# Transposes of four attention slots on 64x64 quarters of TensorE, in another written-out order, in a retention-and-FFN kernel

## The chip, the cores and the metric

The kernel runs on one core of one Trainium2 chip. The metric is the device time of one execution in microseconds; the median of several runs is compared. TensorE is called PE, the loading of its weights PEld, VectorE DVE, ScalarE ACT, GpSimd POOL and SyncE SP, as in the profile.

## What is computed

A causal retention layer is followed by a feed-forward layer. For each of 4 batches and 8 heads (sequence 768, head size 64), with gamma = 1 - 2^(-5-h) for head h:

```python
for t in range(S):
    state = gamma * state + outer(k[t], v[t])
    y[t] = scale * (q[t] @ state)          # scale = 1/8
```

The eight heads of a token side by side are a row x of 512. With 3072 such rows, h = x @ w_in (512 by 2048), g = h * cos(h), and the result is g @ w_out (2048 by 512), in float32.

## The kernel before

The recurrence is done in chunks of 128 tokens. A *slot* p is one chunk of two batches; there are 12 slots, in the order of `ORDER`, and two slots make a *group* of 512 token rows for the FFN (6 groups). A slot goes through these steps:

- *Loads*: q, k and v of the slot, by DMA; those of slots 0 to 7 and the FFN weights (w_in in parts w0a, w0b, w1, w2, w3a, w3b; w_out in o0 to o3) are issued on POOL in the order of the list `LOADS` (q2 is q of slot 2).
- *Conversions* to bf16, with the decay factors multiplied in: q on POOL or DVE (L324, names cq20, cq21 for the two batches of slot 2), k on ACT (L313, ck20), v on POOL or DVE (L336, cv20).
- *Transposes* of q and k, because the scores need the head size on the partitions. Slots 0 to 5 do them on PE (`t_mm`, L361, names t20, t21) and copy them from PSUM to SBUF (`t_copy`, names eq20, ek20); later slots by DMA on SP (`dma_t`, names dt60, dt61). A half u of a slot is four heads, and has one PSUM bank.
- *Scores* (`a_mm`, L389, names a20 and a21 for the two halves of heads in slots 2 and 3, a4; for later slots inside the Y block of the slot before) and their masks (L408).
- *Y block* (`y_block`, L494, L480, L508): scores by v, q by the state, and the update of the state. It is issued on 64x64 quarters of PE, four matmuls side by side. Half of it has to wait for the other half[...]; `told` lets an engine given by `hop_on(p)` wait for the first half and signal the second. That engine is SP for slots up to 4 and POOL after.
- *x copies* (names yc20, yc21) into the 512-row tile `xt`.

The FFN of a group has 16 units of four matmuls (L590, 512 columns; `f_mm`, named f0.3), each followed by a cosine on ACT (L598) and a product on DVE (L602). Where only one slot of a group is ready, half units of 256 columns work on two columns of w_in at once (L611, `h_mm`, named h2.4). `HALF0` is the number of w_in columns of group 0 that are done in half units. `o_mm` (L635) multiplies by w_out.

From slot 6 on the order is a fixed loop (`for g in range(2, NG + 1)`). Before it, in the first 70 us or so, the order of all engines is made at build time by the class `Plan`: each step is added with the engines it may use, its assumed cost, what it follows, a rank, and tokens for PSUM banks and buffers; the plan then steps through time and gives each free engine the ready step of lowest rank. `SHIFT` adds to the ranks of named steps, `ON` limits engines, and both are tables of numbers found by a search. `HOLD` names engines that rather wait than begin a step when one of much lower rank is about to be ready. Where PE would have nothing in the first 18 us, a filler matmul on zeros (L664) is put. The resulting order is emitted instruction by instruction; at run time each engine keeps its order and waits by semaphore.

Of the kernel before, what the change touches and what calls it, by code (L numbers as in the profile page):

```python
# [164 lines left out]
HOLD = ""  # L165
SHIFT = {"ml010": 25.5, "mulf0.2": -74.7, "f0.3": 0.3, "cosf0.2": -11.6, "cosf0.3": -2.2, "mulf0.3": -4.9, "f0.2": 2.8, "m011": -20.0, "mulh1.4": -20.5, "m000": 82.7, "cosf0.5": -41.6, "ck21": 45.1, "a31": -124.5, "m100": 2.2, "f0.5": 23.0, "a5": -2.5, "v0": -97.2, "ms110": 6.4, "ml110": -41.8, "cosf0.4": -0.9, "f0.4": -9.8, "mulf0.5": 16.9, "eq51": 13.1, "m110": 64.4, "t20": -21.1, "k5": -46.0, "mulf0.8": 31.6, "yc21": -50.4, "f0.6": 2.1, "f0.7": 55.3, "ek10": -92.1, "w0b": -22.2, "a21": -34.2, "h1.0": 81.4, "cosh2.2": 3.0, "m501": 38.5, "yc30": -23.3, "ml011": -27.8, "mulf0.15": 5.8, "sc5": 79.1, "m201": -81.3, "mulh2.2": -18.0, "oc1": -45.8, "mulf0.14": -66.8, "cq31": -32.2, "mulf0.9": -47.9, "mulf0.6": 5.7, "cosf0.7": -27.8, "a30": -8.1, "cosf0.6": -7.2, "h0.2": -12.1, "eq21": -4.6, "cq51": 3.2, "cq41": 38.6, "f0.14": 23.8, "ek20": -13.4, "yc50": 39.8, "cv51": 23.4, "ek51": 88.5, "mulh2.10": 23.3, "cq70": 8.6, "f0.10": -46.0, "mulf0.13": 1.5, "h1.6": 5.9, "ml100": 20.1, "f0.15": 60.8, "o2.1": -8.1, "h3.10": 31.9, "t51": 14.8, "h3.0": -7.1, "h3.14": 28.8, "cq00": -2.7, "m601": 4.7, "h1.4": 1.8, "eq11": 37.0, "cosf0.12": -60.7, "v6": -26.4, "m400": 17.7, "mulh3.12": 67.0, "w2": 49.4, "sw": -53.6, "cv10": -0.0, "rv00": 14.5, "mulh2.8": 4.5, "ek50": 72.2, "cosf0.11": 2.4, "m101": -34.4, "h2.2": 1.1, "q2": -22.9, "q5": -59.7, "cosh3.14": 19.9, "y3": 19.8, "t40": 30.7, "o2": -0.8, "mulh3.4": -0.3, "cq40": -13.2, "mulh0.2": -29.3, "y5": -35.7, "mulh3.14": -25.5, "h2.12": -50.9, "oc0": -94.2, "a10": 39.9, "ek11": -35.3, "h0.6": 6.9, "eq40": -6.2, "h2.6": 58.1, "rv10": -9.1, "dt71": -1.3, "cosh3.8": -31.0, "cosh0.2": 18.8, "cv70": -67.6, "o3.1": -13.8, "cq60": -11.1, "ck60": 71.1, "m511": 10.9, "sc4": -15.9, "o1.3": -16.8, "m510": 4.5, "k4": 12.5, "h0.4": -9.2, "cq71": 3.6, "mulh3.2": 58.9, "cosh1.2": -26.7, "mulh3.6": -1.4, "cv61": 13.7, "o2.2": -9.8, "q6": -7.4, "o0.2": -7.5, "mulh2.4": 44.5, "mulh2.6": 22.6, "mulh3.10": 16.6, "v5": -53.7, "cq61": 27.8, "o1.1": -27.2, "ck61": 0.2, "m200": -10.8, "cosf0.9": 6.3, "cosh0.4": 11.6, "q4": 78.9, "cosh3.6": -6.8, "h1.2": -87.9, "tq01": 1.8, "oc3": -74.8, "mulh0.0": -16.9, "eq01": 11.2, "t21": 6.2, "ck41": 29.7, "cosh3.4": 9.3, "oc2": 8.6, "m211": 23.9, "cq01": -56.9, "w0a": 17.8, "o1.0": -7.7, "yc01": 2.2, "k7": 54.8, "yc51": -0.7, "cosf0.13": -14.9, "cosh2.10": -36.4, "yc00": 7.1, "cosh1.4": -13.4, "ek00": -8.7, "m611": -13.9, "tk10": -101.4, "mulh0.4": -40.7, "mulf0.10": 15.2, "m600": -35.2, "a00": -17.4, "cosh2.0": -5.5, "m301": 18.6, "rv11": -50.0, "sc0": -52.0, "ek01": -31.6, "cv01": 13.3, "ek21": -3.2, "cosf0.10": 7.2, "v7": -2.1, "ek40": 18.1, "t31": 22.7, "mulh1.6": 0.2, "eq30": -9.4, "y4": 19.2, "tk11": 1.9, "ek31": -26.9, "w3b": 23.5, "cosh2.12": -0.2, "cosh0.6": 4.7, "cosh2.8": -4.4, "cosh3.2": 25.8, "cv60": 2.7, "cosh2.4": -14.4, "v4": -1.1, "mulh2.12": 36.6, "dt61": -8.8, "eq41": -12.5, "mulf0.11": 31.8, "ek41": -0.8, "eq50": 9.1, "a11": -23.9, "yc10": 9.3, "o0.3": 0.3, "dt60": -3.3, "o3.3": 50.5, "mulh2.14": -42.3, "m610": -12.1, "f0.11": -0.6, "s0": 3.1, "cv11": 38.9, "h3.8": -17.4, "yc40": 14.3, "m410": -8.4, "h2.8": -4.0, "m300": 15.8, "o0": -14.6, "cv31": -27.4, "rv01": 0.6, "cosf0.14": 2.4, "cosh2.6": 11.7, "cv50": -6.8, "m010": -1.2, "ms011": -12.0, "f0.13": -5.2, "l8": 5.1, "ck70": 3.2, "t41": 1.0, "o1.2": -2.3, "cv71": 0.5, "tq11": 31.2, "h2.4": -3.6, "mulh0.6": 8.8, "t50": 7.1, "ck31": 42.7, "yc20": -52.3, "m001": -4.7, "y01": 62.0, "y2": 15.3, "f0.12": 20.5, "ms111": 2.0, "mulh1.2": -13.9, "cosh3.10": -49.0, "ck51": -9.0, "h0.0": -0.1, "eq31": 1.4, "eq20": -5.1, "q7": 1.5, "cosh3.0": 6.2, "cosh3.12": 1.5, "cv40": 2.3, "y11": 3.6, "o1": -24.4, "cv00": -1.4, "sc2": -3.2, "m411": 18.0, "m210": -8.1, "v3": 0.0, "eq10": 1.1, "tk01": 22.8, "yc41": -25.6, "cq21": -1.8, "f0.9": -31.4}
ON = {"cv70": "P", "cv00": "D", "cv30": "D", "cv31": "D", "cv60": "D", "cv11": "D", "cv10": "P", "rv01": "D", "sc5": "D", "rv11": "A", "yc20": "D", "sc3": "D", "eq40": "DA", "eq50": "A", "rv00": "A", "yc00": "D", "yc31": "DA", "ek51": "D", "ek11": "DA", "sc4": "D", "ek20": "A", "cv61": "P", "eq01": "DA", "cv51": "D", "ek41": "D", "eq41": "A", "cv20": "P", "yc01": "DA", "eq20": "A", "eq30": "DA", "ek50": "D", "ek00": "D", "sc2": "DA", "yc50": "DA", "yc40": "A", "yc21": "A", "cq21": "D", "ek40": "DA", "cv01": "D", "cv71": "P", "cv21": "P", "ek21": "DA", "cv41": "P", "cq20": "D", "ek10": "DA", "yc30": "A", "ek01": "D"}
HALF0, SPARE, RF, RM, COLD = 8, 1, 50.0, 50.0, 5.2
# [3 lines left out]
def kernel(  # L172
# [9 lines left out]
    nc = tc.nc  # L182
# [15 lines left out]
    SWAP = 8  # L198
    LATE = NC
# [61 lines left out]
    def qb(p):  # L261
        return by_b(qs[p % NB], p)

    def kb(p):
        return by_b(kx if p == 1 else ks[p % NB], p)
# [89 lines left out]
    def t_mm(p, u, w):  # L355
        if w == 0:
            held["t", p, u] = banks.take()
        tr = held["t", p, u].bitcast(BF16).rearrange("p (w a t) -> p w a t", w=2, a=HP)
        for a in range(HP):
            x = (kb(p) if w else qb(p))  # L360
            nc.tensor.transpose(  # L361
                tr[:, w, a, :],
                x[:, u, 2 * a : 2 * a + 2, :] if p < 2 else x[:, :, 4 * u + a, :], ident)

    def t_copy(p, u, w, e):
        bank = held["t", p, u]
        tr = bank.bitcast(BF16).rearrange("p (w a t) -> p w a t", w=2, a=HP)
        copy(e, qkt[p % NB][:, w, ts(u, HP), :], tr[:, w])
        if w == 1:
            banks.give(bank)  # L370
# [96 lines left out]
    def hop_on(p):  # L467
        return nc.sync if p <= 4 else nc.gpsimd
# [238 lines left out]
    CQ, CD = "P", "DP"  # L707
    SPLIT = {(1, 1, 1), (0, 1, 1)}
    HM, HCQ, HCV = "q2", "", ""
# [9 lines left out]
    LOADS = ["Q1", "K1", "v0", "v1", "w0a", "w0b", "w1", "w2", "q2", "k2", "w3a", "v2", "w3b", "o0", "q3", "k3", "v3", "o1", "q4", "o2", "k4", "v4", "q5", "k5", "o3", "v5", "q6", "k6", "v6", "q7", "k7", "v7"]  # L719
# [28 lines left out]
    for p in range(PL + 2):  # L748
# [26 lines left out]
        if p < DMA_T:  # L775

            for u in range(2):
                cq, ck = ([T["c" + x, p, b] for b in ((u,) if p < 2 else (0, 1))] for x in "qk")
                ev = lambda w, x, need: add("DA", SB2, lambda e, p=p, u=u, w=w: t_copy(p, u, w, e),
                                            need + old, 10 * p + 0.5, (), [("bank", 1)] if w else [],  # L780
                                            name="e%s%d%d" % (x, p, u))
                if p < 2:
                    tq = add("E", 0.225, lambda e, p=p, u=u: t_mm(p, u, 0), cq, 10 * p + 1,
                             [("bank", 1)], (), "full", name="tq%d%d" % (p, u))
                    T["eq", p, u] = ev(0, "q", [tq])
                    tk = add("E", 0.225, lambda e, p=p, u=u: t_mm(p, u, 1), ck + [T["eq", p, u]],
                             10 * p + 1, (), (), "full", name="tk%d%d" % (p, u))
                    T["ek", p, u] = ev(1, "k", [tk])
                else:
                    tq = tk = add("E", 0.45, lambda e, p=p, u=u: (t_mm(p, u, 0), t_mm(p, u, 1)),  # L790
                                  cq + ck, 10 * p + 1, [("bank", 1)], (), "full",
                                  name="t%d%d" % (p, u))
                    T["eq", p, u] = ev(0, "q", [tq])
                    T["ek", p, u] = ev(1, "k", [tk, ("issued", T["eq", p, u])])
                T["tq", p, u], T["tk", p, u] = tq, tk
# [202 lines left out]
```

## Time and profile before

| what | value |
|---|---|
| median of 4 runs | 208.67 us (208.31 to 209.05) |
| profiled execution | 208.43 us, its span 206.6 us |
| PE busy | 201.9 us (98%), 2178 matmuls |
| DVE, ACT, POOL busy | 113.9, 115.5, 73.8 us |
| L635 and L590 matmuls | 368 and 288, 379 ns mean |
| L611 matmuls | 192, 273 ns mean |
| L361 transposes | 96, from 4.3 to 55.9 us |
| L664 fillers | 34, 11.1 us busy |
| mean granted PE clock | 1.000 |

A matmul's duration in the profile includes the pipeline, so matmuls of 379 ns follow each other at 216 ns; what a matmul costs is read from the distance of the starts, or from the pieces of the chain that ended last. "Idle before" names what ended an engine's wait.

### The profile page before, as it was taken

Reading aid. Unit: us, or ns where it says so; the run is one execution under the profiler, and the core shown is the slowest. Engines: PE = TensorE matmul, PEld = TensorE weight load, DVE = VectorE, ACT = ScalarE, POOL = GpSimd, SP = SyncE. Lnnn points to the kernel's source line nnn. Section 1 sums busy time; section 2 is a strip of 40 time slices with the busy share of each in tenths; the row PEclk is TensorE's granted clock in tenths of the full one; section 3 lists DMA queues with packets and bytes.
Section 4 is the critical chain, followed back from the end, with each engine's and each line's share of the span. In section 5 each row is a group of like instructions: output and inputs, shape, how many; then the busy total and the mean of one; then the engine's idle time right before and its main releaser. Section 6 shows DMA issues by size and latency. Waiting matters only on the chain.

```text
span 206.6 us, 5229 instructions
## 1 busy us (share of the span) xinstructions
PE 201.9 (98%) x2178; PEld 109.2 (53%) x2178; DVE 113.9 (55%) x194; ACT 115.5 (56%) x193; POOL 73.8 (36%) x77
## 2 busy tenths in 40 slices
PE   7999999999999999999999999999999999999994
PEld 2548655868945545445445445445444444444442
DVE  4499898865997548338438438448442444444000
ACT  7577787868855357537547547554555553554120
POOL 8879889899973003303303303300000000000000
PEclk9999999999999999999999999999999999999999
DMA  7999999999998974975884776901101101110212
GB/s 119 184 264 213 310 243 309 257 342 277 345 307 148 213 159 110 229 176 140 191 179 130 187 168 157 241 0 56 52 2 51 51 3 51 51 51 0 104 53 102
DMA packets 58600, 32.15 MB, mean 156 GB/s; under 512 B 47696, under 2 KB 53072, under 8 KB 58576
## 3 DMA queue, kind: packets, MB, share of 16 engines
q0 software_dynamic: 14352, 15.47, 33.9%
q1 hardware_dynamic: 44080, 16.28, 31.2%
q8 instruction: 17, 0.28, 0.6%
q10 hardware_dynamic: 144, 0.07, 0.1%
q14 instruction: 7, 0.06, 0.1%
HBM read 27.26 MB, written 6.29 MB: 162 GB/s over the span
## 4 chain that ended last, share of the span: by engine, by line
PE 86%; DMA 8%; POOL 2%; ACT 1%; DVE 1%; issue 1%; POOLq 0%; DVEq 0%; ACTq 0%
PE bank L635 37%; PE bank L590 28%; PE bank L611 7%; DMA kf<-in_k_dram 5%; PE bank L361 3%; PE bank L389 2%; PE bank L664 2%; PE bank L480 2%; DMA qkt<-qs 2%; PE bank L655 2%; PE st_ps L508 2%; DMA qf<-in_q_dram 1%; PE bank L494 1%; POOL am L420 1%; POOL qf L281 1%
## 5 line engine op out<-in xcount | busy, mean ns | idle before, releaser
L598 ACT ACTIVATE cosb<-bank,halfpi 128x512 bf16<-128x512 f32 x96 | 65.5, 689 | 53.8 <-PE bank L590 49.1
L635 PE MATMUL bank<-w_out_sb,gt 128*128 128x512 bf16 x368 | 90.9, 379 | 0.0
L602 DVE TENSOR_TENSOR gt<-bank,cosb 128x512 bf16<-128x512 f32 x72 | 49.0, 689 | 55.8 <-ACT cosb L598 55.7
L590 PE MATMUL bank<-xt,w_in_sb 128*128 128x512 bf16 x288 | 73.2, 379 | 0.0
L635 PEld LDWEIGHTS <-gt 128*128 128x128 bf16 x368 | 35.6, 98 | 42.2
L590 PEld LDWEIGHTS <-w_in_sb 128*128 128x128 bf16 x288 | 27.6, 98 | 32.3
L324 POOL TENSOR_TENSOR qs<-qf,gq 128x512 bf16<-128x512 f32 x18 | 18.5, 1047 | 37.6 <-PE bank L480 37.4
L408 DVE TENSOR_TENSOR am<-bank,mask 128x512 bf16<-128x512 f32 x40 | 24.8, 680 | 4.4 <-PE bank L389 4.4
L313 ACT COPY ob<-bank 128x512 f32<-128x512 f32 (+1 forms) x24 | 14.0, 581 | 16.0 <-PE bank L635 13.9
L611 PE MATMUL bank<-xt,w_in_sb 128*128 128x256 bf16 x192 | 22.3, 273 | 0.0
L611 PEld LDWEIGHTS <-w_in_sb 128*128 128x128 bf16 x192 | 18.5, 98 | 3.1
L619 DVE TENSOR_TENSOR gt<-bank,cosb 128x512 bf16<-128x512 f32 x24 | 16.2, 687 | 5.1 <-ACT cosb L598 4.8
L313 ACT CAST xt<-bank 128x512 bf16<-128x512 f32 x21 | 11.4, 588 | 11.2 <-PE bank L480 10.3
L331 POOL TENSOR_TENSOR vs<-vf,gk 128x512 bf16<-128x512 f32 x8 | 8.2, 1042 | 13.6 <-DMA vf<-in_v_dram 9.1
L313 ACT CAST ks<-kf 128x512 bf16<-128x512 f32 x20 | 11.6, 625 | 2.1 <-DMA kf<-in_k_dram 2.1
L664 PE MATMUL bank<-zero 128*128 128x512 bf16 x34 | 11.1, 461 | 1.1 <-DVE halfpi L680 1.1
L480 PE MATMUL bank<-am,vs 64*64 64x128 bf16 (+1 forms) x320 | 10.3, 206 | 0.1
L336 POOL TENSOR_TENSOR vs<-vf,gk 128x512 bf16<-128x512 f32 x8 | 8.8, 1099 | 2.9 <-PE bank L480 1.4
L281 POOL DMA_DIRECT2D vf<-in_v_dram x8 | 9.4, 1178 | 0.9 <-DVE vs L336 0.8
L315 DVE CAST stb<-st_ps 128x512 bf16<-128x512 f32 x9 | 6.2, 688 | 4.0 <-PE st_ps L508 2.5
L389 PE MATMUL bank<-qkt 64*64 64x128 bf16 (+1 forms) x320 | 7.9, 206 | 0.4 <-DVE qkt L315 0.3
L480 PEld LDWEIGHTS <-vs 64*64 64x64 bf16 x320 | 7.8, 107 | 0.5 <-POOLq L528 0.2
(66 smaller groups left out, 132.0 us busy)
## 6 DMA issues: line engine op xcount, KB each, us to landing
out_dram<-ob SPq DMA_DIRECT2D x23, 256.0 KB, 2.3
vf<-in_v_dram POOLq DMA_DIRECT2D x8, 512.0 KB, 12.2
qf<-in_q_dram POOLq DMA_DIRECT2D x6, 512.0 KB, 12.7
kf<-in_k_dram POOLq DMA_DIRECT2D x6, 512.0 KB, 12.4
w_out_sb<-in_moe_w_out_dram POOLq DMA_DIRECT2D x4, 512.0 KB, 13.6
qf<-in_q_dram SPq DMA_DIRECT2D x4, 512.0 KB, 4.6
w_in_sb<-in_moe_w_in_dram POOLq DMA_DIRECT2D x4, 256.0 KB, 9.1
w_in_sb<-in_moe_w_in_dram POOLq DMA_DIRECT2D x2, 512.0 KB, 10.9
```

The lines of the kernel that those rows point to most:

```text
L313: nc.scalar.copy(out=out, in_=in_)
L324: ENG[e].tensor_tensor(out=qb(p)[:, b], in0=qf[p % PRE][:, b], in1=bc(gq, ORDER[p] % NC), op=ALU.mult)
L389: return nc.tensor.matmul(ap[b][ts(x, 64), a, lo:], lhsT=kt(p % NB, b, h)[:, ts(x, 64)], rhs=qt(p % NB, b, h)[:, lo:], tile_position=(64 * ...
L408: nc.vector.tensor_tensor(out=am[p % 2][b][u], in0=bank.rearrange("p (a t) -> p a t", a=HP), in1=(dec[:, b] if p < 2 else mask[second(p, 0 ...
L480: m = nc.tensor.matmul(held["yp", p][b][ts(j, 64), a, lo:], lhsT=vs[p % NB][ts(r, 64), b, h, :], rhs=am[p % 2][b][h // 4][ts(r, 64), h % 4 ...
L590: nc.tensor.matmul(bank, lhsT=w_in_sb[:, i, ts(f, 128)], rhs=xt[g % 2][:, i, :], start=(i == 0), stop=(i == KIN - 1))
L598: nc.scalar.activation(out=cb, in_=bank, func=AF.Sin, bias=halfpi)
L602: nc.vector.tensor_tensor(out=gt[g % 2][:, f, :], in0=bank, in1=cb, op=ALU.mult)
L611: nc.tensor.matmul(bank[:, ts(e, 256)], lhsT=w_in_sb[:, i, ts(f + e, 128)], rhs=xt[g % 2][:, i, ts(hf, 256)], start=(i == 0 and e == 0), s ...
L619: nc.vector.tensor_tensor(out=gt[g % 2][:, f : f + 2, ts(hf, 256)], in0=bank.rearrange("p (f t) -> p f t", f=2), in1=cb.rearrange("p (f t) ...
L635: nc.tensor.matmul(bank, lhsT=gt[g % 2][:, f, ts(j, 128)], rhs=w_out_sb[:, f, :], start=(f == 0), stop=(f == KOUT - 1))
L664: nc.tensor.matmul(bank[:, : 256 * n].rearrange("p (n t) -> p n t", n=n), lhsT=zero[:, :128], rhs=zero.unsqueeze(1).to_broadcast([128, n, ...
```

## The change

Slots 2 to 5 are transposed on quarters: `t_quad` issues 64 transposes of 64x64 (q and k, 8 heads, 2 batches, 2 halves of the tokens) in place of 16 of 128x128. A half r of its result is now 64 of the 128 tokens for all heads and has one PSUM bank; `t_out` copies it. The plan has one step t2 for what was t20 and t21, it takes two banks at once, and all four copies come before either half of the scores. Slots 0 and 1 keep their full transposes.

With it go new tables for the plan: `SHIFT` and `ON` are replaced as a whole, `HALF0` goes from 8 to 0, POOL is held, the engine of the hop becomes DVE for slots 3, 4 and 5, some loads change places, and another pair of masks of slots 0 and 1 goes to ACT and POOL (`SPLIT`). `HM`, `HCQ` and `HCV` name loads that the plan places after those masks and after slot 2's q and v conversions.

In the order that the build gives, PE then has 2340 matmuls instead of 2179: 64 quarter transposes for 16 full ones in each of four slots, 32 full-width matmuls in place of the 64 half-width ones of group 0, and 35 fillers instead of 34. The order from the first FFN matmul on, with the number of matmuls, is (T full transposes, Q quarter transposes, F L590, H L611, A scores, Y the Y block with its slot, O L635, S the first state):

```
before: H16 S16 H40 F12 H8 F4 T16 F4 A32 F12 Y2 O8 H40 T16 O4 H8 A32 O8 H8 Y3 T16 H64 T16 H8 O4 A32 O16 Y4 O20 Y5 O8 F8 ...
after:  F4 S16 F40 Q64 F8 A32 F12 Y2 O8 H24 Q64 H16 A16 O4 A16 O4 H8 Y3 Q64 O4 H56 O4 Q64 H24 A32 O16 Y4 O16 Y5 O12 F8 ...
```

```diff
-HOLD = ""
+HOLD = "P"
...
-HALF0, SPARE, RF, RM, COLD = 8, 1, 50.0, 50.0, 5.2
+HALF0, SPARE, RF, RM, COLD = 0, 1, 40.0, 50.0, 5.2
...
+    HOP = "SSSDDDP"
...
+    def t_quad(p):
+        bk = [banks.take() for r in range(2)]
+        for r in range(2):
+            held["t", p, r] = bk[r]
+        tr = [t.bitcast(BF16).rearrange("p (w h t) -> p w h t", w=2, h=H) for t in bk]
+        for w in range(2):
+            x = kb(p) if w else qb(p)
+            for h in range(H):
+                for b in range(2):
+                    for r in range(2):
+                        nc.tensor.transpose(
+                            tr[r][ts(b, 64), w, h, :], x[ts(r, 64), b, h, :],
+                            ident[ts(r, 64), ts(r, 64)], tile_position=(64 * r, 64 * b))
+
+    def t_out(p, r, w, e):
+        bank = held["t", p, r]
+        tr = bank.bitcast(BF16).rearrange("p (w h t) -> p w h t", w=2, h=H)
+        copy(e, qkt[p % NB][:, w, :, ts(r, 64)], tr[:, w])
+        if w == 1:
+            banks.give(bank)
...
     def hop_on(p):
-        return nc.sync if p <= 4 else nc.gpsimd
+        return {"S": nc.sync, "P": nc.gpsimd, "A": nc.scalar, "D": nc.vector}[HOP[min(p, 6)]]
...
-    CQ, CD = "P", "DP"
-    SPLIT = {(1, 1, 1), (0, 1, 1)}
-    HM, HCQ, HCV = "q2", "", ""
+    CQ, CD = "P", "P"
+    SPLIT = {(1, 0, 0), (0, 1, 1)}
+    HM, HCQ, HCV = "k2", "q3", "o2"
...
-    LOADS = ["Q1", "K1", "v0", "v1", "w0a", "w0b", "w1", "w2", "q2", "k2", "w3a", "v2", "w3b", "o0", "q3", "k3", "v3", "o1", "q4", "o2", "k4", "v4", "q5", "k5", "o3", "v5", "q6", "k6", "v6", "q7", "k7", "v7"]
+    LOADS = ["Q1", "K1", "v0", "v1", "w0a", "w0b", "q2", "w1", "w2", "k2", "w3a", "v2", "w3b", "o0", "q3", "k3", "v3", "o1", "q4", "k4", "o2", "v4", "q5", "k5", "v5", "o3", "q6", "k6", "v6", "q7", "k7", "v7"]
...
+            if p >= 2:
+                t = add("E", 0.46, lambda e, p=p: t_quad(p), [T["c" + x, p, b] for x in "qk" for b in range(2)],
+                        10 * p + 1, [("bank", 2)], (), "quad", name="t%d" % p)
...
-                    tq = tk = add("E", 0.45, lambda e, p=p, u=u: (t_mm(p, u, 0), t_mm(p, u, 1)),
-                                  cq + ck, 10 * p + 1, [("bank", 1)], (), "full",
-                                  name="t%d%d" % (p, u))
...
-            kq = {u: [T["eq", p, u], T["ek", p, u]] for u in range(2)}
+            kq = {u: [T["e" + x, p, r] for x in "qk" for r in ((u,) if p < 2 else (0, 1))] for u in range(2)}
```

## The prediction

> **What bounds the kernel now.** I read the page's busy shares first, then its slices, the chain that ended last, and then that chain in order of time for the stretch in which slots 2 to 5 are worked.
>
> ```profile
> span 206.6 us, 5229 instructions
> ...
> PE 201.9 (98%) x2178; PEld 109.2 (53%) x2178; DVE 113.9 (55%) x194; ACT 115.5 (56%) x193; POOL 73.8 (36%) x77
> ...
> PE   7999999999999999999999999999999999999994
> ...
> PEclk9999999999999999999999999999999999999999
> ...
> q8 instruction: 17, 0.28, 0.6%
> ...
> PE 86%; DMA 8%; POOL 2%; ACT 1%; DVE 1%; issue 1%; POOLq 0%; DVEq 0%; ACTq 0%
> ```
>
> TensorE (PE) is in work in every slice, at full clock, and no other engine passes 56%. A busy PE is not a useful PE, though: the first 16 us are mostly filler on zeros (L664), and waits of a few tenths hide in the pitch. So a change counts by two things: how much PE work it adds or removes after the first real FFN matmul (15.97 us), and by how much it moves that start or opens a wait. PE's order is fixed; a wait is not filled by other work.
>
> ```profile
> 35.65 4.37 PE bank L611 x40
> 40.02 0.89 PE bank L361 x16
> 40.91 0.86 PE bank L635 x4
> 41.78 0.87 PE bank L611 x8
> 42.65 0.56 PE bank L389 x26
> ...
> 94.46 0.97 PE bank L590 x4
> 95.43 0.86 PE bank L635 x4
> ```
>
> These are the unit prices: 16 full transposes of a slot 0.89 us (56 ns each); a unit of four 512-column matmuls (L590 or L635) 0.86; a half unit (L611) 0.87. The last two rows show what leaving the quarter mode costs: 0.97 against 0.86, so 0.11 to 0.12; start times show 0.09 for entering it. A round trip is 0.21 us.
>
> **The change, part by part.** Counted in the program's order, PE goes from 2179 to 2340 matmuls: 64 quarter transposes for 16 full ones in each of four slots (+192), 32 full-width FFN matmuls for 64 half-width ones (-32), one filler more.
>
> *Quarter transposes.* No transpose in quarters stands in the trace. The nearest rows are the 64x64 matmuls with 64 columns that rotate over the four quarters in a steady block:
>
> ```profile
> 109.21 0.19 PE L389 MATMUL bank<-qkt 64*64 64x64 bf16 x1
> 109.21 0.20 PE L508 MATMUL st_ps<-vs,ks 64*64 64x64 bf16 x2
> 109.22 0.22 PE L389 MATMUL bank<-qkt 64*64 64x128 bf16 x2
> 109.24 0.20 PE L508 MATMUL st_ps<-vs,ks 64*64 64x64 bf16 x2
> 109.27 0.19 PE L389 MATMUL bank<-qkt 64*64 64x64 bf16 x1
> 109.27 0.20 PE L508 MATMUL st_ps<-vs,ks 64*64 64x64 bf16 x2
> 109.28 0.22 PE L389 MATMUL bank<-qkt 64*64 64x128 bf16 x2
> 109.30 0.20 PE L508 MATMUL st_ps<-vs,ks 64*64 64x64 bf16 x2
> 109.33 0.20 PE L480 MATMUL bank<-am,vs 64*64 64x64 bf16 x4
> ```
>
> From 109.21 to 109.33 fourteen start: 8.6 ns each, though each has its own weights. Sixty-four at 8.6 ns are 0.55 us. Floor: 64 columns over four quarters at the 0.434 ns per column of the full transposes (0.89/2048) are 6.9 ns, 0.44 us. Ceiling by a row: the 16 matmuls of L480 with 128 columns at 46.84 (0.41 us, of which the last takes 0.22) start every 12.8 ns, 0.82 us. I take 0.55: saved 0.34 x 4 = 1.36 us, between 1.8 and 0.3.
>
> The Trainium skill speaks against this: "TensorEngine Tiling (Array Packing)", Performance Considerations, Instruction Overhead, gives each matmul about 60 cycles of overhead whatever its width and warns against tiling where the free size is already small. At 0.434 ns per column or cycle that is an estimate of 26 ns, so 1.67 us for a slot and 0.78 lost each: +3.1 instead of -1.4 us. The rows above, at 8.6 ns, decide against reading it as a cost per instruction; overlap of the quarters hides it.
>
> *Mode changes.* Before, PE enters the quarter mode 13 times, after 17: the transposes of slots 2, 3 and 5 stand alone, slot 4's hang on the Y block of slot 3, and the scores of slot 3 are split in two. 4 x 0.21 = +0.86 us. That eats most of the gain.
>
> *HALF0 = 0.* Eight half units become eight full units: 8 x 0.01 = -0.08. But a full unit needs the x of both first slots. Before, L611 starts at 15.97, between them. After, the second group of L431 (15.40 before) has 12 fillers ahead of it since the first scores instead of 16; its last input is a raw-V copy that now stands behind a save and two x copies on ACT. I estimate its start at 15.2 and end at 15.8; behind it stand five fillers at 0.22 and the x copy on DVE, behind one L336 of 1.06: first unit at about 16.9, +0.93 us. It cannot be under 16.4 (copy 0.58 on ACT).
>
> *Load order.* q2 is put ahead of w1. In the trace w0b, w1, w2 and q2 land at 16.57, 19.87, 22.39 and 23.87; q2 takes about 1.5, so w1 lands at 20.7 to 21.4. Four units and the state matmuls (0.47) from 16.9 need it at 20.8: wait 0 to 0.6, taken 0.3. k2 still lands near 25.4, as five loads precede it either way. v5 (1.2 us of issue on POOL) takes the place of o3 (0.78) ahead of the second q conversion of slot 3:
>
> ```profile
> 33.80 1.05 POOL L324 TENSOR_TENSOR qs<-qf,gq 128x512 bf16<-128x512 f32 x1
> 34.79 1.19 POOL L281 DMA_DIRECT2D qf<-in_q_dram  x1
> 35.98 1.15 POOL L281 DMA_DIRECT2D kf<-in_k_dram  x1
> 37.12 0.78 POOL L305 DMA_DIRECT2D w_out_sb<-in_moe_w_out_dram  x1
> 37.89 1.07 POOL L324 TENSOR_TENSOR qs<-qf,gq 128x512 bf16<-128x512 f32 x1
> ```
>
> So that conversion ends near 39.4 instead of 38.96, and slot 3's transposes (16 before at 39.86) start no earlier than 39.5. The later exchanges (o2, o3) are covered: DMA lands a load every 1.5 us until 62.8 both ways.
>
> *Evictions.* Four copies per slot stay (ACT 590 ns, DVE 417). They now split tokens, so the first half of the scores needs all four, not two: 0.5 to 0.6 us later on each engine. Between transposes and scores stand 1.73 to 2.6 us of FFN work, which hides it; with that cover gone it would cost 0.6 once in slot 3.
>
> *Hops of slots 3 to 5 go to DVE* (before: SP for 3 and 4, POOL for 5). Behind them queue masks and products, which wait up to the 0.7 us of half a Y block; DVE has just finished its masks there, so 0, at most 0.7 each. Off SP, the DMA transposes of slot 6 (issued at 62.98, right behind slot 4's hop) go about 0.6 earlier. Before, slot 5's Y block waited for them (376 ns between two starts at 68.22, of which 0.35 is wait): -0.35. The rest (SPLIT, HM, HCQ, HCV, ON, masks to ACT/POOL) moves work among engines below 56% and is costed at nothing beyond the waits named; its cover is the FFN work in between.
>
> *The sum, walked along PE's order.* First unit 16.9; 16 units 13.82, state 0.47, w1 wait 0.3, slot 2's transposes 0.76, scores 0.66: its Y block at 32.9, or 33.3 because DVE's four masks (0.62 each) trail (before 32.43). Y 1.4, four-by-two L635 1.73, three half units 2.62: 39.0, then wait for POOL until 39.5. From there: transposes 0.67, units 1.75, scores 0.44, 0.86, 0.44, 0.86, 0.87, Y block with slot 4's transposes 1.97, 0.86, 6.12, 0.86, slot 5's transposes 0.76, 2.62, scores 0.66, 3.46, Y 1.57, 3.46, Y 1.62: 69.35. Before, that Y block ended at 69.70 with 60 L635 done; after, 56 are, so 0.86 is owed: 70.2 against 69.7, +0.5 us. From there both orders are the same. By cause: -1.36 + 0.86 - 0.08 + 0.93 + 0.3 + about 0.2 (mask and POOL waits after what they absorb) - 0.35.
>
> The profiled execution took 208.43 us, 1.8 around its span of 206.6; the median of the runs is 208.67. Span 207.1, and on the median 209.2 us.
>
> **Rivals.** (1) *Faster.* Transposes at the floor (0.44, -0.44 in all), the first unit at 16.5 and POOL's conversion no later than before (-0.4): 208.2; with the w1 wait gone too, 207.9. For it: PE shows hardly a wait before, and rotation over quarters is the best case. Against: the POOL rows are exact durations, and all must go well together.
> (2) *Slower, by instruction fetch.* PE's code comes in 17 packets of 16 KB (256 instructions, 128 pairs). In the trace each lasts 0.9 to 1.5 us and queues behind the loads. By my prices the blocks of 256 after take 5.4 to 6.3 us each, six in a row from 26 to 67 us; before, two or three were near 5 and the others 6 to 12. "Runtime: NRT & Kernel Launch", Instruction fetch mechanics, calls the crossing mostly hidden because dispatch is slower than the refill: that would be 0 us. The trace is mute on the request; it shows one packet ending at 47.33 and a block before it of about 4.8 us, without a gap in the pitch. It decides once a fetch under load takes over 5.5 to 6 us: three stalls of 0.5 give 210.7.
> (3) *The quarters don't overlap for transposes*: by that page's 26 ns, 209.2 + 4 x (1.67 - 0.55) = 213.7.
> (4) *The change does only half of what it says*: if the scores wait for the later evictions, the transposes' gain is a wait elsewhere: 209.2 + 0.6 = 209.8.
>
> **How the numbers follow.** A measurement of this kernel tells about 0.3%, 0.63 us, from no change. Worked-out case 0.6 (208.5 to 209.9 by the bounds of transposes, start and waits; 0.38 of it within 0.3%, 0.22 above). Rival 1: 0.15 (0.12 faster). Rival 2: 0.15. Rival 3: 0.04. Rival 4: 0.06. Faster 0.12, same 0.41, slower 0.47. Range 207.9 (rival 1 complete) to 210.7 (rival 2); my own case 208.5 to 209.9.
>
> **What would show it.** Right: transposes of a slot start over 0.5 to 0.6 us; first full unit near 16.9; a PE wait ended by POOL before slot 3's transposes near 39; no wait at slot 5's Y block. Wrong: transposes over 0.8 us; gaps of PE inside units, with nothing releasing them, near a packet of the instruction queue; a first unit before 16.5.

## The result and the profile after

The changed kernel takes 209.84 us (median of 39 runs, 209.11 to 210.83) against 208.87 us of the kernel before (58 runs on the same chips, 208.05 to 210.75): ratio 1.0044, 95% interval 1.0033 to 1.0055. That is some 0.9 us slower, and clear of noise; the forecast was 209.2 us, range 207.9 to 210.7. The profiled execution has a span of 207.8 us against 206.6.

First the page of the kernel after: span, busy time, PE's slices and clock, the queue that brings instructions, and the chain that ended last.

```profile
span 207.8 us, 5543 instructions
...
PE 201.9 (97%) x2339; PEld 104.7 (50%) x2339; DVE 113.5 (55%) x192; ACT 116.1 (56%) x195; POOL 73.8 (36%) x77
...
PE   7999899999999999999999999999999999999994
...
PEclk9999999999999999999999999999999999999999
...
q8 instruction: 18, 0.29, 0.6%
...
PE 81%; DMA 11%; POOL 4%; issue 1%; ACT 1%; DVE 0%; POOLq 0%; DVEq 0%
```

PE's busy time is what it was, with 161 matmuls more. In the chain 5% of PE have gone to DMA and POOL. Where they sit is shown by PE's timeline (start, length, line, tiles, shape, count; in brackets the idle time that the profile sees ahead, and what ended it):

```profile
16.72 1.03 PE L613 MATMUL bank<-xt,w_in_sb 128*128 128x512 bf16 x4
17.67 0.44 PE L601 MATMUL st_ps<-vs,ks 128*64 128x64 bf16 x16
18.05 2.76 PE L613 MATMUL bank<-xt,w_in_sb 128*128 128x512 bf16 x12
21.79 6.22 PE L613 MATMUL bank<-xt,w_in_sb 128*128 128x512 bf16 x28 [0.98 <-DMA w_in_sb<-in_moe_w_in_dram]
27.94 0.45 PE L384 MATMUL bank<-ident,qs 64*64 64x64 bf16 x32
28.21 0.46 PE L384 MATMUL bank<-ident,ks 64*64 64x64 bf16 x32
28.61 1.90 PE L613 MATMUL bank<-xt,w_in_sb 128*128 128x512 bf16 x8
...
39.87 0.45 PE L384 MATMUL bank<-ident,qs 64*64 64x64 bf16 x32 [0.32 <-POOL qs L325]
40.14 0.46 PE L384 MATMUL bank<-ident,ks 64*64 64x64 bf16 x32
40.53 1.92 PE L634 MATMUL bank<-xt,w_in_sb 128*128 128x256 bf16 x16
```

Two waits are new: 1.15 us (by start times) for w1 at 21.79, and 0.39 us for POOL ahead of slot 3's transposes. Of the kernel before, these are the start of the FFN and two waits that are shorter now:

```profile
15.97 1.92 PE L611 MATMUL bank<-xt,w_in_sb 128*128 128x256 bf16 x16
29.16 0.64 PE L389 MATMUL bank<-qkt 64*64 64x128 bf16 x32 [0.27 <-DVE qkt L315]
68.59 0.22 PE L389 MATMUL bank<-qkt 64*64 64x128 bf16 x2 [0.16 <-DMA qkt<-qs]
```

The 64 quarter transposes of slot 2 take from 27.94 to 28.61 with the mode exit, so 0.54 us of their own. POOL ahead of 39.87:

```profile
34.04 1.04 POOL L325 TENSOR_TENSOR qs<-qf,gq 128x512 bf16<-128x512 f32 x1 [0.23 <-DMA qf<-in_q_dram]
35.03 1.19 POOL L282 DMA_DIRECT2D qf<-in_q_dram  x1
36.22 1.15 POOL L282 DMA_DIRECT2D kf<-in_k_dram  x1
37.59 1.15 POOL L282 DMA_DIRECT2D vf<-in_v_dram  x1 [0.22 <-issue]
38.76 1.06 POOL L325 TENSOR_TENSOR qs<-qf,gq 128x512 bf16<-128x512 f32 x1
```

Slot 3's second conversion ends at 39.82, and at 38.96 before the change. Three load issues stand ahead of it both ways; of the 0.86 us, 0.24 are the first conversion's later start, as it waits for q3, 0.37 are v5 in place of o3, and 0.22 an idle time ahead of v5's issue.

In the chain that ended last, what leads to slot 3's transposes is POOL, not w1 (start, length, what):

```profile
21.87 12.00 DMA qf<-in_q_dram
34.04 1.04 POOL qs L325
35.08 1.14 POOL qf L282
37.59 1.15 POOL vf L282
38.76 1.07 POOL qs L325
40.60 1.85 PE bank L634 x16
```

Counted along PE, the sum closes. Against before, the first FFN unit starts 0.75 later, w1 costs 1.15 and POOL 0.39; the mode changes add 0.86 (entries 0.093, exits 0.10 to 0.13). The transposes save 4 x 0.355 = 1.42, the full units 0.08, a wait ahead of slot 2's scores 0.33 (0.43 with the entry before, the entry alone after), slot 5's wait for the DMA transposes 0.18 (0.35 became 0.17). Together +1.14. Slot 5's Y block ends at 69.94 instead of 69.70 with one output unit of 0.86 more owed: +1.10. This is a ledger of where PE's time went, not of what each part would give back. Without the wait for w1 PE would have come to slot 3's transposes at 38.33 and stood there until 39.87 for POOL, so that the 1.15 us alone are worth nothing in this execution; this is worked out from the trace and was not run by itself (e1 moves POOL as well).

### The profile page after: what moved, and what is told of

Its sections match the earlier page's. It is cut to its first block, busy times and chain, and to the rows that moved or that the text cites. A ratio compares the mean times of both kernels' runs of the same rounds, so it can differ in the third digit from the quotient of the medians.

```text
span 207.8 us, 5543 instructions
## 1 busy us (share of the span) xinstructions
PE 201.9 (97%) x2339; PEld 104.7 (50%) x2339; DVE 113.5 (55%) x192; ACT 116.1 (56%) x195; POOL 73.8 (36%) x77
## 3 DMA queue, kind: packets, MB, share of 16 engines
HBM read 27.26 MB, written 6.29 MB: 161 GB/s over the span
## 4 chain that ended last, share of the span: by engine, by line
PE 81%; DMA 11%; POOL 4%; issue 1%; ACT 1%; DVE 0%; POOLq 0%; DVEq 0%
PE bank L658 38%; PE bank L613 27%; DMA qf<-in_q_dram 11%; PE bank L634 6%; PE bank L412 2%; PE bank L503 2%; PE bank L678 2%; POOL qs L325 2%; PE st_ps L531 1%; PE bank L687 1%; PE bank L517 1%; PE bank L384 1%; PE bank L362 1%; POOL am L443 1%; POOL vf L282 1%
## 5 line engine op out<-in xcount | busy, mean ns | idle before, releaser
L613 PE MATMUL bank<-xt,w_in_sb 128*128 128x512 bf16 x320 | 80.3, 379 | 1.0 <-DMA w_in_sb<-in_moe_w_in_dram 1.0
L613 PEld LDWEIGHTS <-w_in_sb 128*128 128x128 bf16 x320 | 30.5, 98 | 37.5 <-DMA w_in_sb<-in_moe_w_in_dram 1.7
L325 POOL TENSOR_TENSOR qs<-qf,gq 128x512 bf16<-128x512 f32 x19 | 20.0, 1065 | 44.6 <-DMA vf<-in_v_dram 23.2
L634 PE MATMUL bank<-xt,w_in_sb 128*128 128x256 bf16 x128 | 14.8, 273 | 0.0
L634 PEld LDWEIGHTS <-w_in_sb 128*128 128x128 bf16 x128 | 12.3, 98 | 2.1 <-DVE xt L316 0.2
L332 POOL TENSOR_TENSOR vs<-vf,gk 128x512 bf16<-128x512 f32 x8 | 8.2, 1043 | 6.9 <-DMA vf<-in_v_dram 4.8
L314 ACT COPY qkt<-bank 128x512 bf16<-128x512 bf16 x14 | 7.7, 597 | 2.1 <-PE bank L362 1.2
L337 POOL TENSOR_TENSOR vs<-vf,gk 128x512 bf16<-128x512 f32 x7 | 7.3, 1045 | 3.3 <-PE bank L503 2.2
```

The lines of the kernel that those rows point to most:

```text
L314: nc.scalar.copy(out=out, in_=in_)
L325: ENG[e].tensor_tensor(out=qb(p)[:, b], in0=qf[p % PRE][:, b], in1=bc(gq, ORDER[p] % NC), op=ALU.mult)
L613: nc.tensor.matmul(bank, lhsT=w_in_sb[:, i, ts(f, 128)], rhs=xt[g % 2][:, i, :], start=(i == 0), stop=(i == KIN - 1))
L634: nc.tensor.matmul(bank[:, ts(e, 256)], lhsT=w_in_sb[:, i, ts(f + e, 128)], rhs=xt[g % 2][:, i, ts(hf, 256)], start=(i == 0 and e == 0), s ...
```

## The experiments

Every time below stands beside runs of the kernel before on the same chip. Single executions of one kernel scatter by about 1 us to either side, so a profile shows where time goes and the medians how much. "Row" means the place of an instruction in PE's program, where each matmul is two (weights, matmul); counted from the records of the traces alone, the rows below are 3 or 4 lower, and the gaps again at one place modulo 256. "Pitch" is the usual distance of two starts in the same group.

### e1: w1 ahead of q2 again

```diff
+    at = {o["name"]: o for o in plan.ops}
+    at["q2"]["start"], at["w1"]["start"] = at["w1"]["start"], at["q2"]["start"]
     plan.emit()
```

> The kernel after with two adjacent load issues of POOL exchanged, w1 ahead of q2 (as before the change); everything else stands where it stood. My theory: w1 lands near 20.4 instead of 21.75, so the wait of 1.1 us of L613 at 21.79 goes; k2 still lands near 25.8 and its two conversions on ACT end near 27, so slot 2's transposes start near 27.1 (0.8 earlier); but slot 3's transposes wait for POOL's second q conversion, which ends at 39.8 either way, so they start at 39.87 as before and the time is that of the kernel after, 209.8 us, 0 to -0.2. Rival (the w1 wait alone is what makes the change slower): -1.0 us, 208.8.

Measured: 211.89 us, ratio 1.0146 (1.0112 to 1.0181): 2 us slower than after, which neither theory had. The wait for w1 went, and slot 2's transposes started at 27.16, as expected. But in e1 POOL's conversion of q2 stood like this (first line after, second line e1):

```profile
19.34 1.04 POOL L325 TENSOR_TENSOR qs<-qf,gq 128x512 bf16<-128x512 f32 x1 [0.76 <-DMA qf<-in_q_dram]
```
```profile
21.19 1.54 POOL L325 TENSOR_TENSOR qs<-qf,gq 128x512 bf16<-128x512 f32 x1 [2.33 <-DMA qf<-in_q_dram]
```

POOL stood still for q2 and issued the later loads and conversions some 2 us later. PE's waits of e1, in total, times and longest:

```profile
PE bank L384 <- POOL qs L325: 1.6, 1, 1.6
PE st_ps L531 <- POOL vs L337: 1.2, 1, 1.2
```

So q2 ahead of w1 is no slip: it keeps POOL's queue moving in a plan that converts q2 on POOL. My theory had only looked at the DMA queue. As POOL moved, e1 doesn't tell what the wait for w1 alone is worth.

### e2: slot 3's second conversion behind the first; e3: both edits

```diff
+    at["cq30"]["start"] = at["q5"]["start"] - 0.01
     plan.emit()
```

> The kernel after with one POOL operation moved: slot 3's second q conversion stands directly behind the first, ahead of the issues of q5, k5 and v5. Theory: it ends near 36.2 instead of 39.8, so slot 3's transposes start when PE arrives, 39.45 instead of 39.87: -0.4 us, 209.4. The three loads are issued 1.05 us later and nobody waits for them. Rival (PE would wait there for something else, bank or eviction): no gain, 209.8.

Measured: 209.24 us, ratio 1.0021 (1.0002 to 1.0040), 0.5 us below after by the ratios, where the theory said 0.4; the two intervals just overlap. The wait for POOL is gone. In this execution w1 was no wait either: q2 landed 1.6 us behind the load before it (2.7 in the profile of after), and the FFN began at 17.08. New was a gap of 0.08 us over the pitch inside slot 3's transposes that nothing released.

> Both edits, w1 ahead of q2 and slot 3's second q conversion directly behind the first. Theory: the two waits are in series and the second hides the first, so together they give more than the sum of each alone: slot 2's transposes 0.8 earlier, slot 3's near 38.65 instead of 39.87, -1.2 us, 208.6, level with the kernel before. If gains simply add, -0.4 to -0.6, 209.3; if the time was lost elsewhere (fetch, hops, evictions), 209.6 or more.

Measured: 210.17 us, ratio 1.0058 (1.0036 to 1.0081): not the 208.6 expected. Slot 2's Y block waited 1.4 us, as in e1. Slot 3's transposes, no longer held by POOL, showed a larger gap of that same kind:

```profile
41.00 0.40 PE L384 MATMUL bank<-ident,ks 64*64 64x64 bf16 x28
41.62 0.22 PE L384 MATMUL bank<-ident,ks 64*64 64x64 bf16 x4 [0.21 <-issue]
```

28 of 32 transposes, then 0.4 us between two starts, though all four are ready at once.

### e4: the quarter transposes alone, in the kernel before

```diff
-                    tq = tk = add("E", 0.45, lambda e, p=p, u=u: (t_mm(p, u, 0), t_mm(p, u, 1)),
+                    tq = tk = add("E", 0.45, lambda e, p=p: ("t", p, 0) in held or t_quad(p),
```

(t_quad and t_out are those of after; evictions of slots 2 to 5 call t_out.)

> The kernel before in its own plan, order and loads, with only the transposes of slots 2 to 5 on quarters (64 of 64x64 for 16 full ones) and the four evictions of a slot split by tokens. Theory: 0.34 us saved a slot, 0.21 paid back for a mode round trip in slots 2, 3 and 5 (slot 4's stand directly behind a Y block): 3 x -0.13 and -0.34, sum -0.7 us, of which the wait for evictions ahead of slot 2's scores (0.27 before) may take 0.2: 208.1 to 208.4. Rival (quarter transposes are not cheaper, or code fetch stalls them): 208.9 or more; with 26 ns each, 212.

Measured: 213.59 us, ratio 1.0225 (1.0186 to 1.0263). The transposes are as short as in after, but behind those of slot 4 PE stops:

```profile
47.08 0.45 PE L384 MATMUL bank<-ident,qs 64*64 64x64 bf16 x28
47.34 0.46 PE L384 MATMUL bank<-ident,ks 64*64 64x64 bf16 x32
47.74 0.28 PE L634 MATMUL bank<-xt,w_in_sb 128*128 128x256 bf16 x1
51.39 8.57 PE L634 MATMUL bank<-xt,w_in_sb 128*128 128x256 bf16 x63 [3.37 <-issue]
```

One matmul of a half unit runs, and the next of the same unit 3.65 us later. The row by stages of e4 shows what comes after (window, its length, busy time and count of PE, PEld, DVE, ACT and POOL, granted clock, DMA share, GB/s):

```profile
43.00:47.70 4.70, 4.64 (x173) 3.25 (x164) 4.03 (x7) 2.68 (x5) 4.47 (x5) 1.00 1.03 329
47.70:51.39 3.69, 0.33 (x15) 0.12 (x3) 1.27 (x3) 1.68 (x4) 3.67 (x5) 0.97 1.18 270
51.39:54.40 3.01, 3.01 (x15) 2.09 (x15) 0.61 (x1) 1.33 (x3) 2.99 (x4) 0.50 1.02 343
```

For 3 us PE runs at half clock: matmuls of 256 columns start every 0.214 us instead of 0.109. The gap of 3.54 over the pitch, and 14 x 0.105 for the clock make +5.0; the span grew by 4.4 (211.0 against 206.6), which leaves 0.6 for what the transposes saved.

Then I counted rows. e4's gap lies between rows 1472 and 1474, e3's between rows 961 and 963: one place modulo 512, and a packet of the instruction queue brings some 256 instructions (17 packets for the 4356 rows of the kernel before). This gave a new theory: PE cannot go past a row of 256k - 62 before the packet for the next 256 has come, which starts only when the row before that, 256 back, is passed.

### e5 and e6: the same work, with the boundaries moved

Fillers on zeros are cut into four; that puts more instructions ahead of the same work (26 fillers, 156 rows in e5; 16 fillers, 96 rows in e6):

```diff
-        nc.tensor.matmul(bank[:, : 256 * n].rearrange("p (n t) -> p n t", n=n),
...
+        cut = 4 if idle_no[0] < 26 else 1
+        idle_no[0] += 1
+        for i in range(cut):
+            w = 256 * n // cut
+            nc.tensor.matmul(bank[:, ts(i, w)].rearrange("p (n t) -> p n t", n=n), ...
```

> The kernel before with the quarter transposes (e4), and in addition the first 26 fillers on zeros cut into four matmuls of 128 columns each. The fillers compute nothing that is used and last about as long; but 78 more matmuls (156 instructions) stand ahead of everything, so the boundaries between PE's blocks of 256 instructions fall elsewhere in the same work. Theory (e4's stall of 3.5 us is PE waiting for its next block of instructions, with 1.5 us of half clock behind it): laid over e4's trace with 6.15 us from a boundary to the next block's use, the boundaries now leave one stall of 0.3 us, so the whole of e4's loss but 0.3 goes: 208.5 us (208.2 to 209.2). Rival (the quarter transposes behind a Y block stall for a bank, a semaphore or the mode change): the gap stays where it was, 213.6.

Measured: 209.04 us, ratio 1.0007 (0.9992 to 1.0021). Of e4's loss nearly all is gone. What is left are two gaps at rows 962 and 1986 (0.37 and 0.39) and a smaller one at 1474 (0.16), the wait for evictions ahead of slot 2's scores (0.44) and 0.56 for the DMA transposes in slot 5's Y block.

> The kernel after with the first 16 fillers cut into four matmuls of 128 columns each: 48 more matmuls (96 instructions) ahead of the same work, nothing else. Theory (the plan after the change is slower than it could be only because its blocks of 256 instructions just meet the fetch, and only this alignment does so): by the same model the sixth boundary now falls at 47.7 us, 1.7 us behind the fifth, and PE stalls there 4.5 us and runs at half clock for some 3 us behind it: 209.8 + 4.5 + 1.5 = 215.8 us. Rival (blocks don't matter, the fetch is hidden): 209.8.

Measured: 217.16 us, ratio 1.0400 (1.0374 to 1.0426). The kernel after, shifted by 96 rows, stops where and about as long as the model said:

```profile
48.10 0.43 PE L384 MATMUL bank<-ident,ks 64*64 64x64 bf16 x28
52.93 0.27 PE L384 MATMUL bank<-ident,ks 64*64 64x64 bf16 x4 [4.40 <-issue]
```

The gap lies between rows 1473 and 1475 and is 4.58 us over the pitch, where 4.5 were expected. Behind it PE runs at half clock from 52.93 to about 57.6:

```profile
52.90:56.50 3.60, 3.57 (x16) 1.89 (x17) 2.21 (x3) 1.56 (x3) 2.86 (x3) 0.50 1.05 347
```

The half clock costs 2.2 us by the pitches instead of 1.5. Another wait of 1.1 us stands ahead of slot 1's second matmuls for ACT; as w1 is then waited for less, 0.6 of it are left at slot 2's transposes (28.56 against 27.94). These two make most of the 1.4 us by which the time is over the forecast. The two kernels settle the stall: in one it goes, in the other it appears, with nothing but fillers ahead of the work changed.

Apart from hops, mode changes and single records that a trace lacks, the gaps of PE that nothing releases in slots 2 to 5 all lie on such a row, in every kernel that I ran (those of e5, e9 and e12 at 962, 1474 or 1986). Seven of them, from the traces (times in us; "fetch" is from passing the row 256 back to the next start):

| kernel, row | gap | fetch | packet | packet's end to start |
|---|---|---|---|---|
| e1, 1218 | 0.15 | 6.41 | 45.83 to 46.88 | 1.47 |
| e2, 962 | 0.09 | 5.79 | 37.29 to 38.26 | 1.21 |
| e3, 962 | 0.41 | 6.13 | 39.11 to 40.08 | 1.54 |
| e3, 1218 | 0.23 | 6.47 | 45.59 to 46.56 | 1.53 |
| e4, 1474 | 3.65 | 5.32 | 49.01 to 49.96 | 1.43 |
| e6, 1474 | 4.60 | 6.20 | 50.57 to 51.52 | 1.41 |
| e11, 962 | 0.17 | 5.87 | 37.25 to 38.16 | 1.36 |

And the kernel after, at rows 706, 962, 1218, 1474 and 1730: blocks of 6.04, 6.11, 6.29, 6.36 and 6.29 us, passed 1.42, 1.39, 1.44, 1.59 and 1.78 us behind the packet's end, with no gap above the pitch: five blocks in a row with next to no slack.

The second half of the theory, that a packet starts only when the row 256 back is passed, holds in this stretch and not everywhere. From 100 us on, where the matmuls are long, five of seven packets of the kernel after start 2.6 to 5.1 us before the matmul at that row does (100.80 against 105.00), and in the kernel before the one of row 1474 starts at 59.98 against 61.97. What starts a fetch there stays open.

### e7: full transposes in the plan of after

```diff
-                        nc.tensor.transpose(
-                            tr[r][ts(b, 64), w, h, :], x[ts(r, 64), b, h, :],
-                            ident[ts(r, 64), ts(r, 64)], tile_position=(64 * r, 64 * b))
...
+                    nc.tensor.transpose(tr[:, w, a, :], x[:, :, 4 * u + a, :], ident)
...
```

> The kernel after in its own plan and order, with 16 full transposes per slot in place of the 64 quarter ones in slots 2 to 5 (evictions split by heads). Theory: 0.34 us more a slot, 0.21 less for the mode round trip in slots 2, 3 and 5, with slot 2's 0.13 taken by the wait for POOL ahead of slot 3: +0.13 +0.13 +0.34 = +0.6, 210.4 us. Rival (the quarters are worth nothing in this plan, because the blocks of instructions set the pace from 28 to 59 us and 192 matmuls fewer lift that): 209.5 or less.

Measured: 210.55 us, ratio 1.0096 (1.0077 to 1.0115), over after by 0.7 us by the medians and 1.1 by the ratios. The rival falls: the quarters are worth in this plan about what the unit prices say. In e7 a slot's transposes fill the 0.89 us from 27.89 to 28.78 and w1 is still waited for (0.79). Slot 3's transposes start at 39.91, behind POOL as in after.

### e8: the hops on SP

```diff
-    HOP = "SSSDDDP"
+    HOP = "SSSSSPP"
```

> The kernel after with the hop's engine as before the change (SP for slots 3 and 4, POOL for 5) in place of DVE. Theory: the hop on DVE costs nothing and on SP the same, except that slot 6's DMA transposes stand behind slot 4's hop on SP again: +0.2 at slot 5's Y block (the wait of 0.17 there becomes 0.35), 210.0. Rival (DVE's hop delays masks and products): 209.5 or less.

Measured: 210.56 us, ratio 1.0089 (1.0072 to 1.0106). The direction is right, the size and the reason are not. SP's first DMA transpose of slot 6 now stands ahead of slot 4's hop, starts at 63.83 and holds SP for 1.34 us. Slot 4's Y block waits for the hop behind it, and slot 5's no longer waits for the DMA:

```profile
PE st_ps L531 <- SPq L551: 1.0, 1, 1.0
```

By start times it is 1.20 us. So moving the hops to DVE is worth some 0.7 us to this plan.

### e9, e10 and e12: towards a version faster than both

e9 is e5 with the hops of slots 3 to 5 on DVE; e10 is the kernel before with that edit alone; e12 is e9 with slot 6's first two DMA transposes ahead of an output DMA on SP:

```diff
-        return nc.sync if p <= 4 else nc.gpsimd
+        return {"S": nc.sync, "P": nc.gpsimd, "D": nc.vector}["SSSDDDP"[min(p, 6)]]
...
+    at["dt61"]["start"], at["dt60"]["start"] = at["oc0"]["start"] - 0.02, at["oc0"]["start"] - 0.01
```

> e5 (the kernel before with quarter transposes and 26 fillers cut in four) and in addition the hops of slots 3 to 5 on DVE as in the change. In e5 slot 6's DMA transposes were issued at 63.88 behind slot 4's hop on SP, and slot 5's Y block waited 0.56 us for them. Theory: off SP they go at about 62.8, the wait goes, nothing else changes: 209.0 - 0.5 = 208.5 us, and faster than the kernel before by 0.3. Rival (DVE's hop comes late behind masks): 209.0 or more.

Measured: 208.46 us, ratio 0.9990 (0.9974 to 1.0007). The time is the one expected, but by luck: the wait in slot 5's Y block did not go (0.66 in the profiled execution, which took 210.09). SP's output DMA ahead of the transposes held them (60.61 to 63.46), not the hop.

> Control for e9: the kernel before with nothing but the hops of slots 3 to 5 on DVE. Theory: the wait of 0.35 us of slot 5's Y block for slot 6's DMA transposes goes: 208.5 us. If e9 is no faster than this, the quarter transposes bring nothing even without a stall.

Measured: 208.72 us, ratio 0.9984 (0.9966 to 1.0002). Here the wait is shorter and not gone: 0.22 us by start times (68.68 to 68.93) in place of 0.35.

> e9 with slot 6's two DMA transposes moved on SP ahead of the output DMA of the row block that is written near 62 us. e9 kept its wait (0.66 us at slot 5's Y block) because SP stood behind that output DMA, which waits for ACT's copy, and the transposes came at 63.63 whether the hop was on SP or not. Theory: they are issued near 59.5 as soon as slot 6's conversions are done, the wait goes: 208.5 - 0.6 = 207.9 us, 0.5% below the kernel before. Rival (the transposes, now among the last loads, hold those up or last longer, so the wait stays): 208.5.

Measured: 208.60 us, ratio 0.9987 (0.9966 to 1.0008). The wait of slot 5's Y block is gone, and the median is no lower; why stays open. Its trace has gaps at rows 962 and 1986 (0.31 and 0.27 over the pitch).

All three intervals take in 1. None of these runs shows a version that is faster than the kernel before, and with e10 as control the quarters have brought nothing measurable in the old order. But e5, e9 and e12 have the quarters in the old order and lie below the changed kernel, whose ratio is 1.0044.

### e11: w1 first, with slot 2's conversions moved back

```diff
+    at["cq20"]["start"], at["cq21"]["start"] = at["k3"]["start"] + 0.01, at["mulf0.3"]["start"] + 0.01
```

> The kernel after with w1 issued ahead of q2 and slot 3's second q conversion directly behind the first (as e3), and in addition slot 2's q conversions moved back so that POOL does not stand still for q2: the one on POOL behind the issue of k3, the one on DVE behind the fourth product. Theory: e1 and e3 lost because POOL waited 2.3 us for q2 and passed this to slot 3's loads; without that, slot 2's transposes start near 27.2 and each boundary of blocks 6.2 us behind the last, so the whole stretch comes 0.4 to 0.7 earlier than in e2: 208.6 to 208.9. Rival (POOL's queue is not what cost e1 and e3): 210 or more.

Measured: 209.45 us, ratio 1.0026 (1.0009 to 1.0044): level with e2, not 0.4 to 0.7 below it. The part on POOL holds: against e3, which lacks only this edit, the loss has gone, with no wait for POOL or w1 in the trace. The gain over e2 is missing, and the profiles, one execution of each, show why: e2's had no w1 wait either, and slot 2's transposes start at 27.36 there and 27.34 here. From then on both walk the same row of blocks (30.8 us from row 450 to row 1730).

## Why the prediction was right, and where it was off

- *Quarter transposes.* 0.55 us a slot predicted, 0.54 measured, 8.4 ns each. The 26 ns that the Trainium skill ("TensorEngine Tiling (Array Packing)", Instruction Overhead) would suggest did not appear in transposes that rotate over the quarters. e7 shows the saving in place.
- *Mode changes.* 4 x 0.21: entries and exits are those of before.
- *First FFN unit.* 16.9 predicted, 16.72 measured (17.1 to 17.2 in the profiles of e2, e7, e8 and e11, whose work ahead of it is the same but for loads and hops).
- *w1.* This term was mis-sized: 0 to 0.6, taken 0.3, measured 1.15 in the profile of after, 0.79 in e7, 0.87 in e8, none in e2. I gave q2 the 1.5 us that it took in the middle of the load stream; directly behind w0b it took 2.7 in after, 2.75 in e8, 2.35 in e7 and 1.6 in e2. w1 too took 3.3 us there before the change, and 2.5 behind q2.
- *POOL ahead of slot 3.* Start no earlier than 39.5 predicted, 39.87 measured; wait 0.5 predicted, 0.39 measured. The wait is as forecast only because PE came late as well, 39.48 instead of 39.0. The walk took the start of slot 3's transposes from POOL, and there it is right: the mis-sized wait for w1 is hidden behind POOL. Slot 5's Y block with its owed unit ends at 70.8 where the walk has 70.2; 0.37 of the 0.6 us are POOL's later end, and 0.22 lie in the steps behind it. e2, without the wait for POOL, is 0.5 us faster.
- *Masks.* The walk has slot 2's Y block wait 0.4 us for DVE's masks; it starts at 33.70 with no wait.
- *Evictions.* No wait ahead of the scores of slots 2 and 3; rival 4 did not happen.
- *Hops.* Nothing on DVE, as said. That SP would have cost 1.2 us (e8) the prediction did not see.
- *Slot 5's wait for the DMA transposes.* -0.35 predicted, -0.18 measured.
- *Instruction fetch.* Rival 2 is the point where the prediction knew the mechanism but not its part. It put the decision at 5.5 to 6 us; measured are 5.3 to 6.5 while the loads run. It did not strike because blocks of 6.04 to 6.36 us just clear it, and for the prediction that is luck: 96 rows more ahead of the same work cost over 7 us (e6). The block of 4.8 us that it read in the trace before, ahead of the packet ending at 47.33, is not there by the boundaries found since: that block runs from 43.37 to 49.94. What it would have cost I set at three stalls of 0.5; e4 and e6 show a single stall of 3.5 to 4.6 with half clock behind it. The rule of the Trainium skill, "Runtime: NRT & Kernel Launch", Instruction fetch mechanics, that dispatch is slower than the refill, does not hold here: e4's Y block and transposes passed 256 instructions, from row 1218 to 1474, in 1.7 us (46.07 to 47.74).

The answer to where the transposes' gain went: 1.42 us of it were there, 0.86 went back for mode changes, and the new order lost 0.75 at the start, 1.15 on w1 in this execution and 0.39 on POOL, of which the last two are in series. The old order, which has none of these waits, could not be kept as it stood: with the quarters in it PE stalls (e4). With 26 fillers cut it could: e5 takes what the kernel before takes, less than the new order. The new tables were not tried one by one. Whether the later start (HALF0 = 0, which drops 32 matmuls) is a price of keeping the blocks apart I did not try.

## What to carry to other kernels

Replacing few long instructions by many short ones adds code as well as saving time: count the instructions in the dense stretches, and hold every block of 256 against the time of a fetch under the load that runs there. A gap that nothing releases, inside a run of ready instructions, is tested by cutting fillers ahead of it: if it moves with the count, it is the fetch. And a load put behind another is paid for twice where its consumer sits in an in-order queue that also issues later loads. Ask of two waits in a row whether the second would take up what the first gives back. Take the landing of one load from more than one execution.

## What was not expected of the hardware

- In the kernel after, passing a boundary starts the packet 3.5 to 3.8 us later between 28 and 57 us, while the loads run (3.0 in e4), and 1.0 to 1.6 us later between 64 and 96 us; the packet takes 0.9 to 1.5, and where PE stood for it, it goes on 1.2 to 1.5 us behind its end.
- After a stop of 3.5 us (e4) or 4.6 us (e6) PE is granted half clock, for 3.1 and 4.7 us; after one of 1.8 us (e1, ahead of 41.45) the granted clock stays at 1.00. The Trainium skill, "TensorE: Matmul & The Clock Gate", Part 1, has about 3.4 us of sustained work until the full clock is back; these two lie on either side of it. In the profile's record of the clock, half is granted for 3.41 us in e4 (from 51.15) and 6.83 us in e6 (from 50.90), the ends of the stops included.
